# Cached attention with a gated MLP: steps and sums at other positions, first casts and one weight scaling on ScalarE, final adds but the last on GpSimd

## The chip, the cores and the metric

One core of a Trainium2 chip. The metric is device time of one launch in microseconds; of several runs the median is given. All instructions are written by hand for the five engines: TensorE (PE, with its weight loads as PEld), VectorE (DVE), ScalarE (ACT), GpSimd (POOL) and SyncE (SP), which issues the transfers. They meet only through semaphores, and each engine runs its own list in order: an instruction that waits holds everything behind it on that engine.

## The reference

```python
def _A_ref(x, k_cache, v_cache, wq, wo):          # Sq = Sk = 2048, D = 512, H = 32, Dh = 128
    q = (x @ wq).reshape(B, Sq, H, Dh).transpose(0, 2, 1, 3)
    scores = jnp.einsum("bhqd,bhkd->bhqk", q, k_cache) * (Dh ** -0.5)
    o = jnp.einsum("bhqk,bhkd->bhqd", softmax(scores), v_cache)
    return o.transpose(0, 2, 1, 3).reshape(B, Sq, H * Dh) @ wo

def _B_ref(x, W_gate, W_up, W_down):              # F = 1792
    gate = x @ W_gate
    gate = gate * (gate > 0)
    return (gate * (x @ W_up)) @ W_down

xn = layernorm(A_x)
return A_x + _A_ref(xn, ...) * silu(_B_ref(xn, ...))
```

## The kernel before

The work is 32 heads times 4 query quarters Q of 512 rows: 128 **blocks** b = 4h + Q. A block has 8 **pairs** p of two key tiles of 128. For each pair TensorE makes two score tiles (L1248, "S", 512 columns each) into PSUM, ScalarE takes their exponent in one instruction of 128x1024 (L1260, `PT`), and three pairs later TensorE multiplies `PT` with V (L1357, "PV", eight matmuls of 129 columns, the last column sums the exponents). (b, p) names a place in this sequence. At the end of a block VectorE makes a reciprocal of the sums (L1277) and the normalized output `Onorm` (L1280). The next block's first PV matmul writes the same PSUM banks and waits for that `Onorm`.

PSUM beside the two PV banks is a ring of three slots of two banks. Each S pair takes a slot until its exponent is done. All other products of TensorE ("M items", emitted by `emit_M`) take a slot too, until their results have been read. `plan` says at which (b, p) an M item stands; `side` does the same for VectorE work without TensorE, and `later`/`defer(n, fn)` runs a function n pairs later. These tables, filled by hand-written rules, are the whole order; within one engine the code's order is the run's order.

The M items are:

- `emit_qp` (L815, cast L822): query projections of heads 0 and 1. Those of head 0 stand ahead of the first block, those of head 1 in blocks 0 and 1.
- `emit_st` (L871, VectorE L876, L883): query projections of the later heads, two heads a time (`pr`), in a Strassen scheme of four steps for each half. Its weights are first scaled (L835) and summed (L843 to L848) on GpSimd by `emit_sw(pr)`.
- `emit_gu` (L935, L941): gate and up products of query quarters 1 and 3, in blocks 2 to 12, with weights scaled on ScalarE (L589) and summed on GpSimd (L594 to L599, `SG`). GpSimd also makes ReLU and product of the results (L911, L913).
- `emit_d` (L994, L1003) with sums `emit_hs` (L718 to L727): the down product in four steps, for Q = 1 in blocks 12 and 13.
- `emit_os` (L1131, L1149): output projection of a group g of four heads, four steps for each of four q, in the 16 blocks from b0 = 16(g + 1); sums `emit_ox` (L1100 to L1108, `OX`) feed it. Group 6 is the last one done this way (b0 = 112). Its step 3 also adds two results (L1196, L1198) and hands four output rows of 128 to `base_queue`. `emit_base` (L1225, L1230) then folds gate and residual into them, at the places of `base_at`.
- `emit_final_tile` (L1391): output projection of the last four heads for row tile n = 0 to 15. VectorE multiplies with the gate (L1399), adds (L1415), and SP writes the tile out (L1420). Tiles 0 to 7 stand in blocks 126 and 127, tiles 8 to 15 behind or between the last PV matmuls. The last block's normalization is split by bank (L1300, L1305 on ScalarE, L1311), and its result is transposed on TensorE (L1329).

LB = 124 is the first block of the last head.

Of the kernel before, what the change touches and what calls it, by code (L numbers as in the profile page):

```python
# [8 lines left out]
ALU = mybir.AluOpType  # L9
# [43 lines left out]
def bass_recurrent_scan__mha_block_cached__glu_gated_reglu__prompt_kernel(  # L53
# [35 lines left out]
    WSC = 512.0  # L89
# [26 lines left out]
    with ExitStack() as es:  # L116
# [691 lines left out]
        def emit_qp(h, Q, bank):  # L808
            qs = slice(Q * NQ, (Q + 1) * NQ)
            _wait(pe, wq_tok(0))  # L810
            if h == 0 and Q == 0:
                _wait_all(pe, xt_ready[0])
            ins = None
            for c in range(DC):
                ins = pe.matmul(ps_r[:, bank, :], Wq_sb[0][:, c, h, :], xnT[:, c, qs],  # L815
                                start=(c == 0), stop=(c == DC - 1))
            qtok = sem_qp.sig(ins)
            if h == 1 and Q == QB - 1:
                qp_done_tok[0] = qtok
            dst = qt_take(h, Q)  # L820
            _wait(dve, qtok)
            etok = sem_qpe.sig(dve.tensor_copy(dst, ps_r[:, bank, :]))  # L822
            qt_ready[(h, Q)] = etok
            return etok
# [3 lines left out]
        def emit_sw(pr):  # L828
# [5 lines left out]
            wflat = W[:].rearrange("p c i e -> p (c i e)")  # L834
            k = sem_sw.sig(pool.tensor_scalar(wflat, wflat, WSC, None, op0=ALU.mult))  # L835
            sw_tok[(pr, 0)] = k
# [273 lines left out]
        def emit_os(g, q, step, *banks):  # L1110
# [83 lines left out]
            if g == NG - 2:  # L1194
                _wait_all(dve, [k1, k2])
                t = sem_opa.sig(dve.tensor_tensor(c22, c22, c21, ALU.add))  # L1196
                _wait_all(dve, [t, os_tok[(q, "12")]])
                t = sem_opa.sig(dve.tensor_tensor(c12, c12, c22, ALU.add))  # L1198
                base_queue.extend((m, t) for m in (n, n + 1, NH + n, NH + n + 1))
            return [k1, k2]  # L1200
# [180 lines left out]
        def emit_final_tile(n, bank):  # L1381
# [8 lines left out]
            for hh in range(G):  # L1390
# [8 lines left out]
                dve.scalar_tensor_tensor(fin_tmp[fb], ps_r[:, bank, 0:D], 1.0 / (OSC * YSC), g_sb[:, n, :],  # L1399
                                         op0=ALU.mult, op1=ALU.mult))  # L1400
            flush_final_add()
            fin_pending.append((n, fb, mtok))
            return mtok
# [3 lines left out]
        def flush_final_add():  # L1407
            if not fin_pending:
                return
            n, fb, mtok = fin_pending.pop()  # L1410
            Q, j = divmod(n, 4)
            _wait(dve, mtok)
            _wait(dve, base_done[n])
            ftok = sem_opa.sig(
                dve.tensor_tensor(g_sb[:, n, :], s_acc[:, n, :], fin_tmp[fb], ALU.add))  # L1415
            fin_free[fb] = ftok
# [16 lines left out]
        for g in range(NG - 1):  # L1433
            b0 = (g + 1) * GB
            for i in range(16):
                it = (emit_os, 1 if i % 4 == 3 else 2, g, i // 4, i % 4)
                if g < NG - 2 or i < 10:
                    osteps[b0 + i] = it
                else:
                    at(b0 + 10 + (i - 10) // 2, 4 * (i % 2), it)  # L1440
            for c in range(2):
                for i in range(4):
                    side.setdefault((b0 + 7 * c, 2 + i), []).append((emit_ox, g, c, i))
        gu_n = [len(gu_seq)]

        def gu_items(n):
# [4 lines left out]
        dplan = {2: ((0, 2), (0, 5), (1, 2), (1, 5)),  # L1451
                 1: ((12, 3), (13, 1), (13, 3), (13, 6)),
                 3: ((14, 3), (15, 1), (15, 3), (15, 6))}
# [11 lines left out]
        for b in range(NBLK):  # L1465
# [10 lines left out]
            if 0 < pr < NPR:  # L1476
                c, step = r // 4, r % 4
                q = (emit_st, 1 if step == 3 else 2, pr, c, step)
                first, second = (o, q) if step == 3 and o else (q, o)
                at(b, 0, first)  # L1480
                if second:
# [5 lines left out]
        base_at += [(LB - 1 + k // 2, 2 + k % 2) for k in range(4)]  # L1487
        base_at += [(LB + 1, 1 + k) for k in range(4)]
        for bb, pp in base_at:
# [103 lines left out]
```

## Time and profile before

| | |
|---|---|
| median of 3 runs | 1262.67 us (1262.57 to 1262.78) |
| the profiled execution | 1260.62 us |
| its span, first to last instruction | 1259.3 us |
| busy: PE / ACT / DVE / POOL | 1246.5 / 1018.4 / 686.5 / 275.0 us |
| granted TensorE clock, mean | 0.999 |

A row of the timeline gives start and duration in us, engine, line, operation, tiles, shapes, a count of instructions merged into the row, and in brackets the idle time of the engine ahead of it with what ended it. Matmuls are pipelined: a matmul's duration is longer than the distance to the next one, so rows overlap. Sections of the span: the first gate and up products to about 68 us, attention with the rest of the MLP to about 250 us, attention with projections to 1245 us, and the last tiles behind that.

### The profile page before, as it was taken

What the parts mean: (1) busy time and instruction counts of PE and PEld (TensorE: products, weight loads), DVE (VectorE), ACT (ScalarE), POOL (GpSimd) and SP (SyncE); (2) the same over time, 40 slices, a digit from 0 to 9 for tenths busy, and PEclk for the clock granted to TensorE, in tenths of its full rate; (3) what the DMA queues carried; (4) which work ended last, traced back from release to release, by engine and by line L of the source; (5) the groups of instructions that cost most, each with busy time, mean ns of one, the idle gap of its engine ahead of it and who ended that gap; (6) DMA issues with size and microseconds to landing.
All of it is one profiled execution on the core that took longest, in us unless ns stands there. A gap on an engine that the chain in (4) does not pass through costs nothing.

```text
span 1259.3 us, 28894 instructions
## 1 busy us (share of the span) xinstructions
PE 1246.5 (99%) x12399; PEld 868.8 (69%) x12399; DVE 686.5 (55%) x1174; ACT 1018.4 (81%) x1105; POOL 275.0 (22%) x247
## 2 busy tenths in 40 slices
PE   9999999999999999999999999999999999999998
PEld 5466566777777777777777777777777777777774
DVE  6667677665454444454444545454544454456776
ACT  4356777668888888888888888888888888888884
POOL 2423999510401040100401040102110040100000
PEclk9999999999999999999999999999999999999999
DMA  9712341322223322333222223333223222333212
GB/s 272 154 31 35 70 78 31 51 39 38 44 50 57 68 58 49 60 64 59 52 37 45 59 55 52 60 64 60 52 56 68 56 37 40 52 81 68 68 31 76
DMA packets 250686, 78.02 MB, mean 62 GB/s; under 512 B 226240, under 2 KB 250560, under 8 KB 250560
## 3 DMA queue, kind: packets, MB, share of 16 engines
q1 hardware_dynamic: 249888, 75.79, 31.8%
q8 instruction: 98, 1.61, 0.5%
q10 hardware_dynamic: 672, 0.39, 0.1%
q14 instruction: 28, 0.23, 0.1%
HBM read 38.54 MB, written 2.10 MB: 32 GB/s over the span
## 4 chain that ended last, share of the span: by engine, by line
PE 93%; POOL 2%; DVE 2%; SPq 1%; issue 1%; ACT 1%; DMA 0%; DVEq 0%; POOLq 0%; ACTq 0%
PE ps_acc L1357 36%; PE ps_r L1248 34%; PE ps_r L871 7%; PE ps_r L1131 7%; PE ps_r L935 3%; PE ps_r L994 3%; PE ps_r L656 1%; PE ps_r L660 1%; PE ps_r L815 1%; PE ps_r L1391 1%; POOL hT L913 0%; ACT PT L1260 0%; SPq L521 0%; POOL xn_sb L409 0%; DVE WX L1399 0%
## 5 line engine op out<-in xcount | busy, mean ns | idle before, releaser
L1260 ACT ACTIVATE PT<-ps_r 128x1024 bf16<-128x1024 f32 x1024 | 970.0, 1029 | 170.3 <-PE ps_r L1248 169.8
L1357 PEld LDWEIGHTS ps_acc<-V_sb,PT 128*128 128x128 bf16 x8192 | 604.9, 98 | 220.1 <-ACT PT L1260 18.0
L1357 PE MATMUL ps_acc<-V_sb,PT 128*128 128x129 bf16 x8192 | 749.3, 220 | 1.9 <-DVE Onorm L1280 1.3
L1248 PE MATMUL ps_r<-QT_sb,KT_sb 128*128 128x512 bf16 x2048 | 727.0, 379 | 0.2 <-DVE QT_sb L822 0.2
L1149 DVE TENSOR_TENSOR s_acc<-s_acc,ps_r 128x512 f32<-128x512 f32 x264 | 167.6, 682 | 179.8 <-PE ps_r L1131 179.8
L835 POOL TENSOR_SCALAR Wq_sb<-Wq_sb 128x1024 bf16<-128x1024 bf16 x15 | 41.5, 2769 | 676.1 <-DMA Wq_sb<-in_A_wq_dram 676.1
L1248 PEld LDWEIGHTS ps_r<-QT_sb,KT_sb 128*128 128x128 bf16 x2048 | 187.9, 98 | 1.5 <-DVE QT_sb L822 0.7
L1277 DVE RECIPROCAL rz_sb<-ps_acc 128x4 f32<-128x4 f32 x127 | 23.1, 182 | 199.8 <-PE ps_acc L1357 199.5
L1280 DVE TENSOR_TENSOR Onorm<-ps_acc,rz_sb 128x512 bf16<-128x512 f32 x127 | 87.8, 691 | 4.4
L876 DVE TENSOR_TENSOR QT_sb<-cu,ps_r 128x512 bf16<-128x512 f32 x60 | 41.2, 687 | 85.0 <-PE ps_r L1248 79.8
L871 PE MATMUL ps_r<-xn_sb,SW 128*128 128x512 f16 x180 | 48.6, 379 | 0.0
L1131 PE MATMUL ps_r<-WX,OX 128*128 128x256 f16 x336 | 45.8, 273 | 0.0
L876 DVE TENSOR_TENSOR cu<-cu,ps_r 128x512 f32<-128x512 f32 x60 | 41.2, 687 | 0.0
L1131 PEld LDWEIGHTS ps_r<-WX,OX 128*128 128x128 f16 x336 | 32.9, 98 | 9.8
L876 DVE TENSOR_TENSOR QT_sb<-cv,ps_r 128x512 bf16<-128x512 f32 x60 | 38.3, 680 | 0.0
L1073 POOL TENSOR_SCALAR Wo_sb<-Wo_sb 128x2048 bf16<-128x2048 bf16 x7 | 37.7, 5391 | 0.6
L871 PEld LDWEIGHTS ps_r<-xn_sb,SW 128*128 128x128 f16 x180 | 17.6, 98 | 21.3 <-ACT PT L1260 0.2
L871 PE MATMUL ps_r<-xnT,Wq_sb 128*128 128x512 bf16 x120 | 30.8, 379 | 0.0
L616 ACT ACTIVATE gr_sb<-ps_r 128x512 bf16<-128x512 f32 x27 | 15.7, 593 | 16.7 <-PE ps_r L656 16.0
L1131 PE MATMUL ps_r<-Wo_sb,OT_store 128*128 128x256 bf16 x224 | 29.0, 273 | 0.0
L911 POOL TENSOR_SCALAR gB<-gB 128x512 bf16<-128x512 bf16 x14 | 20.8, 1484 | 32.3 <-DVE gB L941 32.3
L1131 PEld LDWEIGHTS ps_r<-Wo_sb,OT_store 128*128 128x128 bf16 x224 | 21.9, 98 | 8.5
(148 smaller groups left out, 925.1 us busy)
## 6 DMA issues: line engine op xcount, KB each, us to landing
V_sb<-in_A_v_cache_dram SPq DMA_DIRECT2D x32, 512.0 KB, 4.8
Wq_sb<-in_A_wq_dram SPq DMA_DIRECT2D x16, 256.0 KB, 3.3
Wo_sb<-in_A_wo_dram SPq DMA_DIRECT2D x8, 512.0 KB, 3.7
xr_sb<-in_A_x_dram SPq DMA_DIRECT2D x16, 128.0 KB, 2.1
OT_store<-Onorm SPq DMA_TRANSPOSE x127, 2.5
Wd_sb<-in_B_W_down_dram SPq DMA_DIRECT2D x1, 1792.0 KB, 13.6
W<-in_B_W_gate_dram SPq DMA_DIRECT2D x14, 128.0 KB, 2.4
W<-in_B_W_up_dram SPq DMA_DIRECT2D x14, 128.0 KB, 2.8
```

Of the source, the lines that this page charges most:

```text
L835: k = sem_sw.sig(pool.tensor_scalar(wflat, wflat, WSC, None, op0=ALU.mult))
L871: ins = pe.matmul(ps_r[:, bank, :], L(i), R(i), start=(i == 0), stop=(i == HC - 1))
L876: return sem_qpe.sig(dve.tensor_tensor(dst, a, ps_r[:, bank, :], op))
L935: ins = pe.matmul(ps_r[:, bank, :], L(i), R(i), start=(i == 0), stop=(i == HC - 1))
L994: ins = pe.matmul(ps_r[:, bank, j * DH:(j + 1) * DH], L(i), R(i), start=(i == 0 and j == 0), stop=(i == HF - 1 and j == 1))
L1073: k = sem_wx.sig(pool.tensor_scalar(wflat, wflat, WOSC, None, op0=ALU.mult))
L1131: ins = pe.matmul(ps_r[:, bank, j * DH:(j + 1) * DH], L(i), R(i), start=(i == 0 and j == 0), stop=(i == GH - 1 and j == 1))
L1149: t = dve.tensor_tensor(names[k], names[k], view(bank), op)
L1248: ins = pe.matmul(ps_r[:, 2 * s + tt, :], KT_sb[h % 2][:, t * 128:(t + 1) * 128], QT_sb[qt_slot[(h, Q)]][:], start=True, stop=True)
L1260: act.activation(PT[pb][:], ps_r[:, 2 * s:2 * s + 2, :], ACTF.Exp, scale=scale if h < 2 else scale / WSC)
L1280: dve.tensor_tensor(Onorm[ob][:], o_ap, rz_sb[:].to_broadcast([128, 4, Dh]), ALU.mult))
L1357: ins = pe.matmul(o_ap, PT[pb][:, tt, j * 128:(j + 1) * 128], V_sb[vb][:, t, 0:VW], start=(t == 0 and j % 2 == 0), stop=(t == KT - 1 and j ...
```

## The change

Eight edits. Head 0's projections of Q = 1 and 3 are cast on ScalarE instead of VectorE. The scaling of the weights of pr = 2 moves from GpSimd to ScalarE. The last group's two result sums (L1196, L1198) are deferred by one pair. Its steps of q = 3 stand at (123, 0), (124, 0), (125, 0), (125, 4) instead of (123, 0), (123, 4), (124, 0), (124, 4). `emit_ox` of the second half starts one pair earlier in every group. In block 13 the down product's second step changes place with the projection step: (13, 0) and (13, 2) instead of (13, 1) and (13, 0). The last four base sums stand at (125, 6), (125, 7), (126, 2), (126, 6) instead of (125, 1) to (125, 4). The final adds run on GpSimd, except that of tile 15, and directly behind their own multiply instead of behind the next one.

```diff
@@ emit_qp
-            _wait(dve, qtok)
-            etok = sem_qpe.sig(dve.tensor_copy(dst, ps_r[:, bank, :]))
+            if h == 0 and Q % 2 == 1:
+                _wait(act, qtok)
+                etok = sem_gua.sig(act.copy(dst, ps_r[:, bank, :]))
+            else:
+                _wait(dve, qtok)
+                etok = sem_qpe.sig(dve.tensor_copy(dst, ps_r[:, bank, :]))
@@ emit_sw
-            k = sem_sw.sig(pool.tensor_scalar(wflat, wflat, WSC, None, op0=ALU.mult))
+            if pr == 2:
+                _wait(act, wq_tok(pr))
+                k = sem_w2s.sig(act.activation(wflat, wflat, ACTF.Copy, scale=WSC))
+            else:
+                k = sem_sw.sig(pool.tensor_scalar(wflat, wflat, WSC, None, op0=ALU.mult))
             sw_tok[(pr, 0)] = k
             _wait(pool, k)
@@ emit_os, step 3
             if g == NG - 2:
-                _wait_all(dve, [k1, k2])
-                t = sem_opa.sig(dve.tensor_tensor(c22, c22, c21, ALU.add))
-                _wait_all(dve, [t, os_tok[(q, "12")]])
-                t = sem_opa.sig(dve.tensor_tensor(c12, c12, c22, ALU.add))
-                base_queue.extend((m, t) for m in (n, n + 1, NH + n, NH + n + 1))
+                def finish():
+                    ...
+                defer(1, finish)
@@ emit_final_tile, flush_final_add
+            fin_pending.append((n, fb, mtok))
             flush_final_add()
-            fin_pending.append((n, fb, mtok))
...
-            _wait(dve, mtok)
-            _wait(dve, base_done[n])
-            ftok = sem_opa.sig(
-                dve.tensor_tensor(g_sb[:, n, :], s_acc[:, n, :], fin_tmp[fb], ALU.add))
+            eng, sem = (dve, sem_opa) if n == NT - 1 else (pool, sem_hp)
+            _wait(eng, mtok)
+            _wait(eng, base_done[n])
+            ftok = sem.sig(eng.tensor_tensor(g_sb[:, n, :], s_acc[:, n, :], fin_tmp[fb], ALU.add))
@@ the tables
-                    at(b0 + 10 + (i - 10) // 2, 4 * (i % 2), it)
+                    at(b0 + (10, 10, 11, 12, 13, 13)[i - 10], 4 * (i in (11, 15)), it)
...
-                    side.setdefault((b0 + 7 * c, 2 + i), []).append((emit_ox, g, c, i))
+                    side.setdefault((b0 + 7 * c, (2, 1)[c] + i), []).append((emit_ox, g, c, i))
...
-                 1: ((12, 3), (13, 1), (13, 3), (13, 6)),
+                 1: ((12, 3), (13, 0), (13, 3), (13, 6)),
...
-                at(b, 0, first)
+                at(b, 2 if b == 13 else 0, first)
...
-        base_at += [(LB + 1, 1 + k) for k in range(4)]
+        base_at += [(LB + 1, 6), (LB + 1, 7), (LB + 2, 2), (LB + 2, 6)]
```

The changed kernel's lines are numbered 8 higher than the old ones from L843 on and 10 higher from L1225 on. First place: VectorE in blocks 124 to 126. Before, from the last two results of group 6 on; `Onorm_75` is block 124's output, `Onorm_76` that of block 125, L1225 and L1230 are one base sum:

```order
L1149 TENSOR_TENSOR s_acc_111<-s_acc_111,ps_r 128x2x256 x2
L1196 TENSOR_TENSOR s_acc_111<-s_acc_111 128x2x256
L1198 TENSOR_TENSOR s_acc_111<-s_acc_111 128x2x256
L1277 RECIPROCAL rz_sb_73<-ps_acc 128x4
L1280 TENSOR_TENSOR Onorm_75<-ps_acc,rz_sb_73 128x512
L1225 TENSOR_SCALAR s_acc_111<-s_acc_111,g_sb 128x512
L1230 TENSOR_TENSOR s_acc_111<-s_acc_111,xr_sb_116 128x512
```

and now, up to block 126's first two final tiles (L1409 is the old L1399):

```order
L1287 RECIPROCAL rz_sb_73<-ps_acc 128x4
L1290 TENSOR_TENSOR Onorm_75<-ps_acc,rz_sb_73 128x512
L1157 TENSOR_TENSOR s_acc_111<-s_acc_111,ps_r 128x2x256 x5
L1205 TENSOR_TENSOR s_acc_111<-s_acc_111 128x2x256
L1207 TENSOR_TENSOR s_acc_111<-s_acc_111 128x2x256
L1235 TENSOR_SCALAR s_acc_111<-s_acc_111,g_sb 128x512
L1240 TENSOR_TENSOR s_acc_111<-s_acc_111,xr_sb_116 128x512
L1235 TENSOR_SCALAR s_acc_111<-s_acc_111,g_sb 128x512
L1240 TENSOR_TENSOR s_acc_111<-s_acc_111,xr_sb_116 128x512
L1287 RECIPROCAL rz_sb_73<-ps_acc 128x4
L1290 TENSOR_TENSOR Onorm_76<-ps_acc,rz_sb_73 128x512
L1409 TENSOR_SCALAR WX_115<-ps_r,g_sb 128x512 x2
```

The results of q = 3 and their sums have moved behind block 124's output, and two base sums now stand ahead of block 125's. In the part before, four base sums and then block 125's reciprocal follow the rows shown.

Second place: ScalarE in block 4, from the scaling of gate and up weights into `W_67` to that into `W_68`. Before:

```order
L589 ACTIVATE W_67_84<-W_67_84 128x1024
L1260 ACTIVATE PT<-ps_r 128x1024 x4
L589 ACTIVATE W_68_85<-W_68_85 128x1024
```

and now (L1270 is the old L1260):

```order
L589 ACTIVATE W_67_84<-W_67_84 128x1024
L1270 ACTIVATE PT<-ps_r 128x1024 x2
L841 ACTIVATE Wq_sb<-Wq_sb 128x1024
L1270 ACTIVATE PT<-ps_r 128x1024 x2
L589 ACTIVATE W_68_85<-W_68_85 128x1024
```

The scaling stands between the second and the third exponent; on GpSimd its place between the sums `SG_87` and `SW_79` is now empty.

Third place: VectorE from tile 8's multiply to the end of the last block's normalization. Before:

```order
L1399 TENSOR_SCALAR WX_115<-ps_r,g_sb 128x512
L1415 TENSOR_TENSOR g_sb<-s_acc_111,WX_115 128x512
L1399 TENSOR_SCALAR WX_115<-ps_r,g_sb 128x512
L1415 TENSOR_TENSOR g_sb<-s_acc_111,WX_115 128x512
L1300 RECIPROCAL rz_sb_73<-ps_acc 128x2 x2
L1311 TENSOR_TENSOR Onorm_78<-ps_acc,rz_sb_73 128x256
```

and now from tile 4's multiply to VectorE's end, with the six adds between tile 4 and tile 9 gone:

```order
L1409 TENSOR_SCALAR WX_115<-ps_r,g_sb 128x512 x6
L1310 RECIPROCAL rz_sb_73<-ps_acc 128x2 x2
L1321 TENSOR_TENSOR Onorm_78<-ps_acc,rz_sb_73 128x256
L1409 TENSOR_SCALAR WX_115<-ps_r,g_sb 128x512 x6
L1425 TENSOR_TENSOR g_sb<-s_acc_111,WX_115 128x512
```

More of the change, by code (lines that the diff above doesn't have):

```diff
@@ L1194, in emit_os @@
             if g == NG - 2:
-                _wait_all(dve, [k1, k2])
-                t = sem_opa.sig(dve.tensor_tensor(c22, c22, c21, ALU.add))
-                _wait_all(dve, [t, os_tok[(q, "12")]])
-                t = sem_opa.sig(dve.tensor_tensor(c12, c12, c22, ALU.add))
-                base_queue.extend((m, t) for m in (n, n + 1, NH + n, NH + n + 1))
+                def finish():
+                    _wait_all(dve, [k1, k2])
+                    t = sem_opa.sig(dve.tensor_tensor(c22, c22, c21, ALU.add))
+                    _wait_all(dve, [t, os_tok[(q, "12")]])
+                    t = sem_opa.sig(dve.tensor_tensor(c12, c12, c22, ALU.add))
+                    base_queue.extend((m, t) for m in (n, n + 1, NH + n, NH + n + 1))
+                defer(1, finish)
             return [k1, k2]
```

## Prediction

> **What bounds the kernel now.** I read the page first, then who waited for whom on TensorE, then the timeline around each of those waits.
>
> ```profile
> span 1259.3 us, 28894 instructions
> PE 1246.5 (99%) x12399; PEld 868.8 (69%) x12399; DVE 686.5 (55%) x1174; ACT 1018.4 (81%) x1105; POOL 275.0 (22%) x247
> PE ps_r L935 <- POOL SG L599: 3.0, 1, 3.0
> ```
>
> TensorE is the bound nearly everywhere. Busy alone would not say so, as matmuls overlap; that its waits are few and short does. The change touches no product, so all it can win is idle time of TensorE ahead of its last matmul and the tail behind it. What counts is therefore each single wait, and what comes late next once it is gone.
>
> One rule for reading them. A 512-column matmul is shown as 0.38 us, but four take 1.03 (second row below), so they start every (1.03 - 0.38) / 3 = 0.216 us. An idle time in brackets starts only where the modelled end lies; the loss is larger by 0.38 - 0.216 = 0.16. I add 0.16 to each bracket.
>
> **First casts.**
>
> ```profile
> 70.43 2.47 DVE L822 CAST QT_sb<-ps_r 128x512 bf16<-128x512 f32 x4
> 71.74 1.03 PE L1248 MATMUL ps_r<-QT_sb,KT_sb 128*128 128x512 bf16 x4
> 72.37 2.86 ACT L1260 ACTIVATE PT<-ps_r 128x1024 bf16<-128x1024 f32 x3 [4.32 <-PE ps_r L1248]
> 72.96 1.09 PE L1248 MATMUL ps_r<-QT_sb,KT_sb 128*128 128x512 bf16 x4 [0.20 <-DVE QT_sb L822]
> 74.36 0.82 PE L815 MATMUL ps_r<-xnT,Wq_sb 128*128 128x512 bf16 x3 [0.31 <-ACT PT L1260]
> L616 ACT ACTIVATE gr_sb<-ps_r 128x512 bf16<-128x512 f32 x27 | 15.7, 593 | 16.7 <-PE ps_r L656 16.0
> ```
>
> The third S pair waits 0.36 us for four casts that run one behind the other to 72.90; a first exponent starts at 72.37, one PE-to-engine step of 0.41 behind the second S tile (71.74 + 0.216). With Q = 1 and 3 on ScalarE (0.59 each by L616) that wait goes: Q = 2 ends on VectorE before 71.8 and Q = 3, whose last matmul starts 0.216 ahead of S, runs 71.93 to 72.52; S wants the slot at 72.60. But the projections at 74.36 wait for the second exponent, and exponents follow each other on ScalarE. Q = 3's cast now stands ahead of the first one and lets it start at about 72.42. So the chain from the first exponent decides, TensorE waits 0.36 us less at one place and more at the next two, and the sum is **+0.05** (0 to +0.15).
>
> **The scaling of pr = 2.**
>
> ```profile
> Wq_sb<-in_A_wq_dram SPq DMA_DIRECT2D x16, 256.0 KB, 3.3
> 129.46 0.58 SPq L335 DMA_DIRECT2D Wq_sb<-in_A_wq_dram  x1
> 131.50 2.18 ACT L1260 ACTIVATE PT<-ps_r 128x1024 bf16<-128x1024 f32 x2
> 134.53 1.02 ACT L1260 ACTIVATE PT<-ps_r 128x1024 bf16<-128x1024 f32 x1 [0.86 <-PE ps_r L1248]
> L589 ACT ACTIVATE W<-W 128x1024 bf16<-128x1024 bf16 x14 | 14.8, 1057 | 3.2 <-DMA W<-in_B_W_up_dram 3.2
> 136.11 2.77 POOL L835 TENSOR_SCALAR Wq_sb<-Wq_sb 128x1024 bf16<-128x1024 bf16 x1
> 138.97 0.67 POOL L843 TENSOR_TENSOR SW<-Wq_sb 128x256 f16<-128x256 bf16 x1
> 149.79 0.38 PE L935 MATMUL ps_r<-xn_sb,SG 128*128 128x512 f16 x1 [3.03 <-POOL SG L599]
> ```
>
> The one large wait is 3.19 us. GpSimd's list runs without a gap from before 136 to the sums (`SG`) that TensorE wants at 149.79 - 3.19 = 146.60, so every microsecond taken out of it arrives there whole. What goes is L835 with its semaphore, 138.97 - 136.11 = 2.86. That leaves a wait of 0.33. On ScalarE the scaling has the shape of L589, 1.06 us, and stands behind the second exponent, which ends at 131.50 + 2.18 = 133.68, in a hole of 0.86; the pitch of such instructions is about 0.1 shorter than their duration, so the next exponent is late by 0.1 at most, and its reader comes three pairs later. Its data land at 129.46 + 3.3 = 132.8, 0.9 us early; a later landing would hold up the exponents behind it, which are then wanted by the ring within a microsecond. The cost on ScalarE I take at nothing, **-2.86** in all (-3.19 to -1.9, the end where landing slips by a microsecond).
>
> **Block 13.**
>
> ```profile
> 231.01 3.22 PE L994 MATMUL ps_r<-Wd_sb,hT 128*128 128x256 bf16 x28
> 237.33 1.16 DVE L727 TENSOR_TENSOR HS_sb<-hT,HS_sb 128x1024 f16<-128x1024 f16 x1
> 237.91 1.11 POOL L844 TENSOR_TENSOR SW<-Wq_sb 128x256 f16<-128x256 bf16 x1
> 238.62 0.69 DVE L1280 TENSOR_TENSOR Onorm<-ps_acc,rz_sb 128x512 bf16<-128x512 f32 x1
> 239.46 0.61 PE L1357 MATMUL ps_acc<-V_sb,PT 128*128 128x129 bf16 x8 [0.38 <-DVE Onorm L1280]
> ```
>
> PV can start 0.84 behind the start of `Onorm` (238.62 to 239.46), and two projection matmuls cover too little: 0.54 us lost. Now 28 down matmuls (3.06 us) stand there, and the wait goes. What is late next is the ring: the projection at (13, 2) and the down step at (13, 3) lie in neighbouring pairs, and the latter takes the slot of the S pair just ahead. From that S pair's second tile to the down step TensorE has 0.216 + 0.43 + 0.45 + 0.43 = 1.53 us of other work, an exponent needs 0.41 + 1.02 and a further 0.26, since the pair before it, without an M item, ends its S only 0.66 earlier and exponents follow each other by 0.92 ((2.86 - 1.02) / 2 by the row at 72.37). So 0.2 comes back: **-0.33** (-0.54 to 0).
>
> **`OX` a pair earlier, sums a pair later.**
>
> ```profile
> 1171.79 1.28 DVE L1149 TENSOR_TENSOR s_acc<-s_acc,ps_r 128x512 f32<-128x512 f32 x2 [1.73 <-PE ps_r L1131]
> 1174.44 0.68 DVE L1105 TENSOR_TENSOR OX<-OX,OT_store 128x1024 f16<-128x1024 f16 x1
> 1175.16 0.69 DVE L1108 TENSOR_TENSOR OX<-OT_store,OX 128x1024 f16<-128x1024 bf16 x1
> 1176.82 0.39 PE L1357 MATMUL ps_acc<-V_sb,PT 128*128 128x129 bf16 x4 [0.66 <-ACT PT L1260]
> ```
>
> This wait of 0.82 is put down to an exponent, but VectorE's list ran without a gap up to the `Onorm` that PV needs. L1105 now falls into the idle 1.73 ahead of L1149, which takes 1175.16 - 1174.44 = 0.72 out of the list, and the pause of a dependent step (0.12) goes between L1105 and L1108. The reciprocal then comes no later than the PV results allow: **-0.8** (-0.82 to -0.7).
>
> **Blocks 124 to 126.**
>
> ```profile
> 1214.78 0.60 PE L1131 MATMUL ps_r<-WX,OT_store 128*128 128x256 f16 x4
> 1217.49 0.69 DVE L1198 TENSOR_TENSOR s_acc<-s_acc 128x512 f32<-128x512 f32 x1
> 1218.53 0.18 DVE L1277 RECIPROCAL rz_sb<-ps_acc 128x4 f32<-128x4 f32 x1 [0.34 <-PE ps_acc L1357]
> 1219.35 0.68 DVE L1225 SCALAR_TENSOR_TENSOR s_acc<-s_acc,g_sb 128x512 f32<-128x512 f32 x1
> 1219.58 0.39 PE L1357 MATMUL ps_acc<-V_sb,PT 128*128 128x129 bf16 x4 [0.88 <-DVE Onorm L1280]
> 1220.68 0.68 DVE L1225 SCALAR_TENSOR_TENSOR s_acc<-s_acc,g_sb 128x512 f32<-128x512 f32 x1
> 1226.44 0.59 PE L1248 MATMUL ps_r<-QT_sb,KT_sb 128*128 128x512 bf16 x2
> 1228.60 0.62 PE L1357 MATMUL ps_acc<-V_sb,PT 128*128 128x129 bf16 x8
> ```
>
> Block 125 starts with no M item, so TensorE waits the bare 1.04 us for `Onorm`. Now eight matmuls of group 6 stand there, as at the other block ends, and this goes: -1.04. But the last step, with its sums, moves from (124, 4) to (125, 4), and two base sums now stand between these sums and block 125's reciprocal. Counted from the last step's first matmul (1214.78 before), the sums' second add starts 2.71 later and ends its turn at 3.43; two base sums take 2 x (1220.68 - 1219.35) = 2.66; the reciprocal comes at 6.1 instead of 3.75, PV may start 1.05 behind it, at 7.15 (1218.53 to 1219.58). TensorE reaches block 126's S at 3.55 and its PV, past the first two final tiles, 1228.60 - 1226.44 = 2.16 later, at 5.71. So a **new wait of about 1.4 us** stands at the start of block 126. The edit gives -1.04 + 1.4 = **+0.4** (-1.04 if VectorE gets through in time, +0.6 if it takes 0.2 longer).
>
> **The last tiles.**
>
> ```profile
> 1249.57 0.38 PE L1329 MATMUL ps_r<-ident,Onorm 128*128 128x128 bf16 x4 [0.60 <-ACT Onorm L1305]
> 1243.74 0.69 DVE L1399 SCALAR_TENSOR_TENSOR WX<-ps_r,g_sb 128x512 bf16<-128x512 f32 x1 [2.78 <-PE ps_r L1391]
> 1250.85 0.69 DVE L1399 SCALAR_TENSOR_TENSOR WX<-ps_r,g_sb 128x512 bf16<-128x512 f32 x1 [0.43 <-PE ps_r L1391]
> 1256.26 1.28 DVE L1415 TENSOR_TENSOR g_sb<-s_acc,WX 128x512 bf16<-128x512 f32 x2
> 1257.57 0.33 SPq L1420 DMA_DIRECT2D out_dram<-g_sb  x1
> L913 POOL TENSOR_TENSOR hT<-gA,uA 128x512 f16<-128x512 bf16 x14 | 16.2, 1155 | 1.2
> ```
>
> The transposes wait 0.76 us for the last normalization, which waits on VectorE behind two multiplies and two adds; without the adds (0.60 of list each, 1.28 less 0.68, what such a step takes by L1225) it starts up to 1.2 earlier, and the wait goes: -0.76. Behind it VectorE is the bound today: 16 multiplies and 16 adds by turns. Now the multiplies keep TensorE's pace, one tile in 4 x 0.216 = 0.865 us, and GpSimd adds. The trace has no f32 add on GpSimd; nearest is L913, the same 512 columns in two-byte types, 1.155 (pitch 1.13). Below that nothing speaks; above, if bytes set the price, a 1024-column add in two-byte types, extrapolated from 0.67 for 256 columns and 1.155 for 512, is 2.13. I take 1.13, since rates seem to go by columns. Tile 11's multiply, at 1250.85 - 0.76 = 1250.09, ends at 1250.8; four adds (11 to 14) end at 1255.3. Tile 15's add on VectorE reads two SBUF tensors, as L727 did above when it took 1.16 and L844 beside it 1.11 instead of 0.67; I add 0.3 for that. SP then issues tile 14 (0.33) and about 0.4 later tile 15, at 1256.1 instead of 1257.57: -1.5 for both, thus **-0.7** for the tail beyond the transposes (+1.4 at 1.48, +7.3 at 2.13).
>
> The Trainium skill speaks against this edit: its page "GPSIMD Engine Reference", section "Engine selection", puts elementwise work on VectorE, with GpSimd about half as fast in two-input adds. The rows agree on the price (1.155 against 0.68); going by the rule, the adds would stay and the 0.7 be lost, but here it is two lists side by side against one.
> The same page, section "Specifications", says that GpSimd shares its SBUF interfaces with VectorE when that reads two SBUF inputs. The rows L727 and L844 agree; nothing here shows whether a multiply that reads one of its inputs from PSUM is free of it, but L913's mean of 1.155 was taken while such combines ran on VectorE.
>
> **Sum.** 0.05 - 2.86 - 0.33 - 0.8 + 0.4 - 0.76 - 0.7 = -5.0 us against the profiled span of 1259.3, thus 1254.3, or 1255.6 for a profiled execution (1260.6 with what lies around the span). The median of the runs is 2.05 above that execution; I carry the difference to it: 1262.67 - 5.0 = **1257.7**. About 0.2% of it, 2.5 us, is what a measurement of this kernel can tell from no change.
>
> **Rivals.**
>
> *All waits go, none comes (11%).* Block 125's reciprocal would not stand behind the base sums in time, nor the ring hold the down step. For it: the list has slack at other block ends. Against it: the order on VectorE and the pitch of 1.33 a base sum. -5.0 - 1.4 - 0.2 = -6.6: 1256.1.
>
> *GpSimd's large gain is half eaten (12%).* `Wq_sb` lands a microsecond later than before, or the sums wait for something the long wait hid; exponents queue behind the scaling. TensorE then keeps 1 to 2 us of the 3.2. For it: a margin of 0.9 on one transfer. -5.0 + 1.5: 1259.2.
>
> *The adds on GpSimd become the end (6%, slower).* If f32 is paid by bytes, 2.13 each. From tile 6 on, whose multiply ends at 1243.74 + 0.69, nine adds end at 1263.6; 0.4 and the last transfer's 1.73 (1257.57 to the span's end) put the end at 1265.8, 6.5 later than today; with -3.5 from the edits before it this is +3.0: 1265.7. It decides from 1.8 us an add on for no gain, 2.1 for slower by 0.2%. Against it: L913's price, and that two-byte types of different kinds cost it the same. A middle price of 1.5 gives 1259.9.
>
> *The waits are not where the trace says (6%).* Each goes, and TensorE meets the exponents instead, as in the first edit: ScalarE is busy 81%. For it: brackets naming `PT`. Then -1 to -2: about 1261.
>
> **How the numbers follow.** My forecast with all its terms has 65%. Time 1257.7. The range, 1255.6 to 1260.6, holds it and the first two rivals and ends where GpSimd's add costs 1.6 or one term of 2.9 fails. Slower by over 0.2% is most of the third rival: 0.05. Within 0.2% are the fourth and what is left of the third and second: 0.09. Faster: 0.86.
>
> **What would show it.** In the profile after: no 3 us wait at L935 but one of 0.2 to 0.4; no wait at the first PV of blocks 13, 120 and 125 above 0.2; a new one of about 1.2 in the bracket at block 126's first PV, released by `Onorm`; the projections behind the first S pairs waiting for `PT` 0.7 to 0.9 in two steps; GpSimd's last adds at 1.1 to 1.2 us; the last transfer issued 5 us earlier. Adds of over 1.5 us, or a first-PV wait at block 126 that is missing, would make the sum wrong; exponents late around the moved scaling would make the largest term wrong.

## The result, and the profile after

| | before | after |
|---|---|---|
| median, six runs each | 1262.58 us (1261.37 to 1262.78) | 1256.28 us (1255.73 to 1256.70) |
| profiled execution / its span | 1260.62 / 1259.3 us | 1255.73 / 1254.1 us |

The changed kernel is faster: the ratio is 0.9951, with an interval of [0.9939, 0.9964]. The prediction was 1257.7 us, faster with 0.86. Its sum for the span was -5.0 us; the two spans differ by 5.2. The median fell by 6.3, and the 1.1 between the two is the most useful thing that this case has to show.

First the page of the changed kernel, then who waited for whom on TensorE (in total, times, longest, in us):

```profile
span 1254.1 us, 28671 instructions
PE 1234.5 (98%) x12173; PEld 868.8 (69%) x12399; DVE 681.7 (54%) x1157; ACT 1020.3 (81%) x1108; POOL 290.3 (23%) x261
PE ps_acc L1367 <- DVE Onorm L1290: 1.3, 1, 1.3
PE ps_r L815 <- ACT PT L1270: 0.3, 1, 0.3
PE ps_r L943 <- POOL SG L599: 0.2, 1, 0.2
```

TensorE's busy time can't be compared with before's: 226 of its matmul records are missing here (12,173 beside 12,399 weight loads). Its waits can. The 3.0 us for `SG` are down to 0.2, and the list is led by a wait for `Onorm`, at a place (block 126) where before had none. The timeline at the places that the prediction named, with the add of 0.16 to each bracket as there:

```profile
72.31 3.78 ACT L1270 ACTIVATE PT<-ps_r 128x1024 bf16<-128x1024 f32 x4
73.40 0.61 PE L1258 MATMUL ps_r<-QT_sb,KT_sb 128*128 128x512 bf16 x2 [0.25 <-ACT PT L1270]
74.31 1.04 PE L815 MATMUL ps_r<-xnT,Wq_sb 128*128 128x512 bf16 x4 [0.31 <-ACT PT L1270]
133.52 1.05 ACT L841 ACTIVATE Wq_sb<-Wq_sb 128x1024 bf16<-128x1024 bf16 x1
146.91 0.38 PE L943 MATMUL ps_r<-xn_sb,SG 128*128 128x512 f16 x1 [0.20 <-POOL SG L599]
241.55 0.38 PE L1258 MATMUL ps_r<-QT_sb,KT_sb 128*128 128x512 bf16 x1
241.99 0.28 PE L1002 MATMUL ps_r<-Wd,HS_sb 128*128 128x256 f16 x1
1221.28 0.69 DVE L1235 SCALAR_TENSOR_TENSOR s_acc<-s_acc,g_sb 128x512 f32<-128x512 f32 x1
1223.94 0.18 DVE L1287 RECIPROCAL rz_sb<-ps_acc 128x4 f32<-128x4 f32 x1
1224.99 0.61 PE L1367 MATMUL ps_acc<-V_sb,PT 128*128 128x129 bf16 x8 [1.25 <-DVE Onorm L1290]
```

Of the places in question, these waits are left: 0.41 and 0.47 for the first exponents, 0.36 for `SG`, 0.22 at block 13's down step (0.44 from the S tile ahead of it instead of 0.22), and 1.41 at block 126, where VectorE runs from 1221.28 without a gap through two base sums to the reciprocal. None is left at the first PV of blocks 13, 120 and 125, nor at the transposes. The end, where GpSimd now adds:

```profile
1246.16 5.60 POOL L1425 TENSOR_TENSOR g_sb<-s_acc,WX 128x512 bf16<-128x512 f32 x5 [0.77 <-DVE WX L1409]
1249.93 0.69 DVE L1409 SCALAR_TENSOR_TENSOR WX<-ps_r,g_sb 128x512 bf16<-128x512 f32 x1 [0.17 <-PE ps_r L1401]
1250.66 1.65 DVE L1425 TENSOR_TENSOR g_sb<-s_acc,WX 128x512 bf16<-128x512 f32 x1
1243.19 9.48 SPq L1430 DMA_DIRECT2D out_dram<-g_sb  x7
```

Five adds in 5.60 us are 1.12 each, as priced. The last add on VectorE took 1.65 us, not the 0.98 of the prediction.

### The profile page after: what moved, and what is told of

Same layout as the page of the kernel before. It is cut to its first block, busy times and chain, and to the rows that moved or that the text cites. A ratio compares the mean times of both kernels' runs of the same rounds, so it can differ in the third digit from the quotient of the medians.

```text
span 1254.1 us, 28671 instructions
## 1 busy us (share of the span) xinstructions
PE 1234.5 (98%) x12173; PEld 868.8 (69%) x12399; DVE 681.7 (54%) x1157; ACT 1020.3 (81%) x1108; POOL 290.3 (23%) x261
## 4 chain that ended last, share of the span: by engine, by line
PE 84%; ACT 10%; POOL 2%; issue 1%; SPq 1%; DVE 1%; DMA 0%; POOLq 0%; DVEq 0%; ACTq 0%
PE ps_acc L1367 34%; PE ps_r L1258 28%; ACT PT L1270 10%; PE ps_r L1139 6%; PE ps_r L879 6%; PE ps_r L943 3%; PE ps_r L1002 3%; PE ps_r L656 1%; PE ps_r L660 1%; PE ps_r L1401 1%; PE ps_r L815 1%; POOL hT L921 0%; SPq L521 0%; POOL xn_sb L409 0%; POOL gB L919 0%
## 5 line engine op out<-in xcount | busy, mean ns | idle before, releaser
L1270 ACT ACTIVATE PT<-ps_r 128x1024 bf16<-128x1024 f32 x1024 | 969.9, 1028 | 161.2 <-PE ps_r L1258 149.7
L1258 PE MATMUL ps_r<-QT_sb,KT_sb 128*128 128x512 bf16 x1831 | 652.7, 379 | 2.0 <-ACT PT L1270 0.2
L1157 DVE TENSOR_TENSOR s_acc<-s_acc,ps_r 128x512 f32<-128x512 f32 x264 | 167.7, 683 | 178.1 <-PE ps_r L1139 178.1
L843 POOL TENSOR_SCALAR Wq_sb<-Wq_sb 128x1024 bf16<-128x1024 bf16 x14 | 38.8, 2771 | 675.9 <-DMA Wq_sb<-in_A_wq_dram 675.9
L1425 POOL TENSOR_TENSOR g_sb<-s_acc,WX 128x512 bf16<-128x512 f32 x15 | 17.8, 1216 | 153.9 <-DVE WX L1409 153.9
```

What stands on the lines that cost most here:

```text
L1157: t = dve.tensor_tensor(names[k], names[k], view(bank), op)
L1258: ins = pe.matmul(ps_r[:, 2 * s + tt, :], KT_sb[h % 2][:, t * 128:(t + 1) * 128], QT_sb[qt_slot[(h, Q)]][:], start=True, stop=True)
L1270: act.activation(PT[pb][:], ps_r[:, 2 * s:2 * s + 2, :], ACTF.Exp, scale=scale if h < 2 else scale / WSC)
```

## Experiments

To compare traces I use one number throughout: the span less the start of the first exponent (1254.1 - 72.31 = 1181.8 for the changed kernel, 1259.3 - 72.37 = 1186.9 for before). It leaves out the part ahead of attention, in which one wait differs from execution to execution (more on it below). The spans are given to 0.1 us, so a difference of two of these numbers is good to about 0.1. Two profiles of the changed kernel agree that closely. The first casts stand partly ahead of this number's start, so they are read from the first S matmul instead.

| run | span less first exponent | median | before in the same comparison |
|---|---|---|---|
| before (first profile) | 1186.93 | | |
| before again | 1188.63 | 1263.04 | 1262.49 |
| before, wait filled | 1186.97 | 1261.32 | 1263.06 |
| after (first profile) | 1181.79 | 1256.28 | 1262.58 |
| after again | 1181.82 | 1256.96 | 1262.99 |
| scaling back on GpSimd | 1184.61 | 1260.62 | 1262.49 |
| casts back on VectorE | 1181.72 | 1256.59 | 1263.06 |
| `OX` back | 1182.40 | 1256.89 | 1263.06 |
| final adds back on VectorE | 1183.30 | 1257.55 | 1262.49 |
| base sums late | 1180.26 | 1255.12 | 1262.49 |
| last product in PSUM | 1181.66 | 1256.43 | 1263.06 |
| base sums late, two products in PSUM | 1179.83 | 1254.16 | 1262.99 |
| the same, sums of pr = 2 in block 8 | 1181.49 | 1255.70 | 1262.99 |

### Before, profiled again

No edit.

> The kernel before, unchanged, profiled a second time. The changed kernel's median is 6.3 us lower (1262.58 to 1256.28), but the spans of the two profiled executions differ by 5.2 only (1259.3 to 1254.1), and before's profiled execution (1260.62) lies 2.0 under its median while after's (1255.73) lies 0.6 under it. Theory: that 1.2 is no part of the change; this run's profile then shows the same single waits as the first one (3.19, 1.04, 0.82, 0.76, 0.54 us, each within 0.1), whatever its time is, and a longer execution is longer in the stretches between them or at the start. Rival: one of the waits is longer in an ordinary execution than in the one that was read (the 3.19 us above all, which hangs on GpSimd's list); its wait then shows 4 to 5 us here in an execution near 1262.5.

It was 1.70 us longer behind the first exponent, and the same waits stand there within 0.02 us. The windows (stretch, its length, busy time of PE, PEld, DVE, ACT and POOL, then the granted clock of TensorE, DMA share and GB/s) and TensorE's rows behind the 3.2 us wait:

```profile
151.00:153.00 2.00, 1.59 (x4) 0.59 (x5) 0.54 (x1) 0.00 (x0) 1.92 (x3) 0.59 0.00 0
153.00:155.00 2.00, 2.00 (x12) 1.27 (x11) 0.83 (x2) 0.01 (x1) 2.00 (x2) 0.55 0.00 0
155.00:157.00 2.00, 2.00 (x23) 1.40 (x22) 1.58 (x3) 1.05 (x2) 1.92 (x3) 1.00 0.00 0
151.41 1.87 PE L935 MATMUL ps_r<-xn_sb,SG 128*128 128x512 f16 x4 [3.04 <-POOL SG L599]
153.07 1.07 PE L1357 MATMUL ps_acc<-V_sb,PT 128*128 128x129 bf16 x8
154.79 0.60 PE L935 MATMUL ps_r<-xn_sb,SG 128*128 128x512 f16 x2
```

From 151.41 to about 154.8 the clock is halved: the four products take 1.87 us here and 1.02 in before's first profile, whose windows behind the same wait are at full clock:

```profile
149.79 1.02 PE L935 MATMUL ps_r<-xn_sb,SG 128*128 128x512 f16 x4 [3.03 <-POOL SG L599]
151.00:153.00 2.00, 2.00 (x20) 1.24 (x18) 1.63 (x4) 1.02 (x1) 1.92 (x3) 1.00 0.00 0
153.00:155.00 2.00, 2.00 (x23) 1.40 (x21) 1.23 (x3) 1.29 (x2) 1.92 (x3) 1.00 0.00 0
```

Half the clock for 3.4 us loses 1.7, which accounts for the 1.70. The other 1.6 us between the two spans (1262.6 and 1259.3) are the start-up of the last section.

So my theory was right that the waits are the same and the rival wrong that one is longer; but the surplus does lie at the wait, right behind it. The times of before show it as two groups. Of the 21 in this comparison ten lie from 1260.9 to 1261.6 at a mean clock of 0.999 to 1.000, eleven from 1262.5 to 1264.2 at 0.997 or 0.998. The profile that I read the sum from was of the lower group, the median of the upper.

### Before, with the wait filled

```diff
+            if (k, m) == (5, 6):
+                for _ in range(13):
+                    pe.matmul(ps_r[:, bank, :], W[:, 0, 0, :], xnT[:, 0, lo], start=True, stop=True)
             if m == 6:
                 _wait(pe, gu_tok[(k, "x")])
```

> The kernel before with 13 more matmuls of 512 columns in its 3.2 us wait, written to the bank that the waiting product overwrites: the wait is as long, but TensorE is busy for 2.8 us of it. The 21 times of before in the last comparison fall into two groups, ten from 1260.9 to 1261.6 and eleven from 1262.5 to 1264.2, and the second profile of before, a run of the upper group, shows a granted clock of 0.59 and 0.55 in the 3.4 us behind this wait. Theory: the idle time itself brings the clock down in about half of the executions, for 1.6 us. With TensorE kept busy the upper group is gone: every time within 1 us, a median near 1261.2, 1.3 under before. Rival: the clock drops there for another reason, or the groups come from the start-up: both groups stay, and the median is that of before.

```profile
146.55 2.97 PE L924 MATMUL ps_r<-xnT,W 128*128 128x512 bf16 x13
149.68 1.04 PE L938 MATMUL ps_r<-xn_sb,SG 128*128 128x512 f16 x4 [0.16 <-POOL SG L599]
151.00:153.00 2.00, 2.00 (x20) 1.17 (x17) 1.62 (x4) 1.02 (x1) 1.92 (x3) 1.00 0.04 8
```

The products start as late as ever, with 2.8 us of work that nobody needs ahead of them, and the median is 1261.32 against 1263.06 us, a ratio of 0.9991. Its interval, [0.9982, 1.0000], just reaches no change; the two groups tell more. Nine of its eleven times lie from 1260.6 to 1261.6. A tenth, 1262.45, ran at a clock of 1.000, so it lost its time elsewhere. The eleventh, 1264.11 at 0.998, looks like the upper group and stays unexplained. In before, ten of 14 on the same chip were above 1262.8. So it is the idle time that brings the clock down in nearly all of these executions; the one exception is open.

The Trainium skill, page "TensorE: Matmul & The Clock Gate", section "What's actually happening", has the array drop to half its clock after an idle window of about 3.4 us, by windows that run freely, and come back after one such window of work. Half the clock for 3.4 us and only in some executions agree with the rows above. The length does not: here 3.0 to 3.2 us of idle time were enough in more than half of the executions, and by the page's length there would have been no loss.

### The scaling back on GpSimd

```diff
-            if pr == 2:
-                _wait(act, wq_tok(pr))
-                k = sem_w2s.sig(act.activation(wflat, wflat, ACTF.Copy, scale=WSC))
-            else:
-                k = sem_sw.sig(pool.tensor_scalar(wflat, wflat, WSC, None, op0=ALU.mult))
+            k = sem_sw.sig(pool.tensor_scalar(wflat, wflat, WSC, None, op0=ALU.mult))
```

> The changed kernel with only the scaling of pr = 2 back on GpSimd. Theory: GpSimd's list has no gap from block 4 on, so 2.77 us and its semaphore arrive whole at the sums that TensorE waits for: the wait of 0.37 at the gate and up products becomes 3.2, the time rises by 2.8 us against the changed kernel (3.5 us under before). Rival: about half of the gain was eaten by ScalarE (exponents behind the scaling): then the 3.2 us wait is back, but the time rises by 1.3 to 2 only.

```profile
151.02 1.02 PE L939 MATMUL ps_r<-xn_sb,SG 128*128 128x512 f16 x4 [3.03 <-POOL SG L599]
```

The wait is 3.19 us again, and the profile 2.82 us longer than the changed kernel's (1184.61 - 1181.79). The rival, ScalarE eating half of the gain, is out. With the wait the wide spread is back: eleven times from 1258.9 to 1262.7 at clocks from 0.997 to 1.000, where kernels without it stay within 1.3 us.

### The first casts back on VectorE

```diff
-            if h == 0 and Q % 2 == 1:
-                _wait(act, qtok)
-                etok = sem_gua.sig(act.copy(dst, ps_r[:, bank, :]))
-            else:
-                _wait(dve, qtok)
-                etok = sem_qpe.sig(dve.tensor_copy(dst, ps_r[:, bank, :]))
+            _wait(dve, qtok)
+            etok = sem_qpe.sig(dve.tensor_copy(dst, ps_r[:, bank, :]))
```

> The changed kernel with all first casts back on VectorE. Theory: the chain of exponents decides there, not the casts; the 0.36 us wait for a cast is back, but the waits for the first exponents shrink by as much, and the four products of TensorE end at the same time within 0.1 us: no change of time that can be measured (0.05 less). Rival: the wait for the cast was the loss that the trace names: 0.36 us more, seen as a later start of the projections behind the first S pairs.

```profile
72.45 1.03 PE L1254 MATMUL ps_r<-QT_sb,KT_sb 128*128 128x512 bf16 x4
73.67 1.09 PE L1254 MATMUL ps_r<-QT_sb,KT_sb 128*128 128x512 bf16 x4 [0.20 <-DVE QT_sb L822]
75.08 0.60 PE L815 MATMUL ps_r<-xnT,Wq_sb 128*128 128x512 bf16 x2 [0.31 <-ACT PT L1266]
```

From the first S matmul to the projections there are 75.08 - 72.45 = 2.63 us; in the changed kernel 74.31 - 71.63 = 2.68, from the S row that comes first there:

```profile
71.63 1.52 PE L1258 MATMUL ps_r<-QT_sb,KT_sb 128*128 128x512 bf16 x6
```

The wait for a cast is back and nothing is lost. It was never a cost of its own: the same time is waited for an exponent instead. By these two rows the edit is worth +0.05, which is too little to be told from nothing.

### `OX` back

```diff
-                    side.setdefault((b0 + 7 * c, (2, 1)[c] + i), []).append((emit_ox, g, c, i))
+                    side.setdefault((b0 + 7 * c, 2 + i), []).append((emit_ox, g, c, i))
```

> The changed kernel with the sums OX of the second half of each group one pair later again, as before. Theory: VectorE's list, with these two sums in it, makes block 119's normalized output late; the wait of 0.82 us at block 120's first PV is back, and the time rises by 0.8 us. Rival: the wait there was for an exponent, as its row in the trace says, and went for another reason: no change. In the six earlier groups the sums have slack either way in both theories.

```profile
1172.32 0.69 DVE L1207 TENSOR_TENSOR s_acc<-s_acc 128x512 f32<-128x512 f32 x1
1172.93 0.17 DVE L1287 RECIPROCAL rz_sb<-ps_acc 128x4 f32<-128x4 f32 x1
1173.14 0.69 DVE L1290 TENSOR_TENSOR Onorm<-ps_acc,rz_sb 128x512 bf16<-128x512 f32 x1
1173.97 0.61 PE L1367 MATMUL ps_acc<-V_sb,PT 128*128 128x129 bf16 x8 [0.54 <-ACT PT L1270]
```

The wait is back with 0.70 us, and the time behind the first exponent is 0.61 longer. The row still names an exponent, but VectorE reaches the reciprocal without a gap and PV starts 0.83 behind the start of `Onorm`, as at block 13 before (0.84). The second profile of before settles it: there the same wait, with the same 0.66 in the bracket, is put down to `Onorm`:

```profile
1180.07 0.61 PE L1357 MATMUL ps_acc<-V_sb,PT 128*128 128x129 bf16 x8 [0.66 <-DVE Onorm L1280]
```

The name in the first profile's bracket was wrong, the list of VectorE right.

### The base sums late

```diff
-        base_at += [(LB + 1, 6), (LB + 1, 7), (LB + 2, 2), (LB + 2, 6)]
+        base_at += [(LB + 2, 1), (LB + 2, 2), (LB + 2, 6), (LB + 3, 2)]
```

> The changed kernel with the last four base sums at (126, 1), (126, 2), (126, 6) and (127, 2) instead of (125, 6), (125, 7), (126, 2) and (126, 6). Theory: the 1.42 us in front of block 126's first PV are the two base sums (2 x 1.33) that stand ahead of block 125's reciprocal on VectorE; without them the reciprocal starts at about 1222.0 in place of 1223.9 and the wait goes: 1.4 us less than the changed kernel. Rival: the reciprocal is held by the late step of group 6 (its four adds and two sums, which end at 1221.25) or by contention with GpSimd's adds in block 126; then the wait shrinks by half at most or comes back as 0.5 us or more at block 127's first PV: 0.7 us less or nothing.

```profile
1222.11 0.18 DVE L1287 RECIPROCAL rz_sb<-ps_acc 128x4 f32<-128x4 f32 x1 [0.37 <-PE ps_acc L1367]
1224.07 0.62 PE L1367 MATMUL ps_acc<-V_sb,PT 128*128 128x129 bf16 x8
```

The reciprocal now waits for TensorE, not TensorE for it, and block 126's PV has no wait: 1.53 us less, against a wait of 1.41 that is gone. The two base sums were the whole new wait.

### The final adds back on VectorE

```diff
-            fin_pending.append((n, fb, mtok))
             flush_final_add()
+            fin_pending.append((n, fb, mtok))
...
-            eng, sem = (dve, sem_opa) if n == NT - 1 else (pool, sem_hp)
+            eng, sem = dve, sem_opa
```

> The changed kernel with all final adds back on VectorE, each behind the next tile's multiply as before. Theory: the transposes wait 0.76 us again, and the chain of multiplies and adds on VectorE ends 0.8 us later behind TensorE's last matmul (4.2 us lay between that and the span's end in the changed kernel, 5.0 before): 1.6 us more than the changed kernel. The four base sums' adds in blocks 126 and 127, stretched to 1.0 to 1.5 us beside GpSimd's adds, return to 0.68 without a gain. Rival: the slowing that VectorE and GpSimd do to each other (0.68 to 1.65 at the last add) eats most of what the two lists win side by side; then the time rises by 0.6 us or less.

```profile
1246.51 0.38 PE L1339 MATMUL ps_r<-ident,Onorm 128*128 128x128 bf16 x4 [0.60 <-ACT Onorm L1315]
```

The transposes wait 0.76 us again, and the span behind the first exponent is 1.51 longer. The theory held, and contention ate little. This run undoes the engine and the order of the adds together; what each is worth alone was not tried. About 0.3 us of the gain is lost again outside the span (last section).

### The last product in PSUM

The main lines of the edit, shortened:

```diff
-                dve.scalar_tensor_tensor(fin_tmp[fb], ps_r[:, bank, 0:D], ...
+                dve.scalar_tensor_tensor(ps_r[:, bank, 0:D] if n == NT - 1 else fin_tmp[fb], ps_r[:, bank, 0:D], ...
...
+                                            last_bank[0] if n == NT - 1 else fin_tmp[fb], ALU.add))
```

> The changed kernel with the last tile's product left in PSUM in f32 instead of SBUF in bf16, so that VectorE's last add reads one of its inputs from PSUM. Theory: this add took 1.65 us in place of 0.68 because it reads both inputs from SBUF beside GpSimd's adds; with one in PSUM it takes 0.69 and ends at 1251.35 on the changed kernel's scale, and GpSimd's add of tile 14 (1251.76, perhaps 0.1 sooner) becomes the last: 0.4 to 0.6 us less in the time. Rival: GpSimd's traffic slows any VectorE instruction that reads f32 from SBUF; then the add takes 1.3 us or more and the time falls by 0.3 at most.

```profile
1249.49 2.26 POOL L1427 TENSOR_TENSOR g_sb<-s_acc,WX 128x512 bf16<-128x512 f32 x2
1250.66 0.69 DVE L1427 TENSOR_TENSOR g_sb<-s_acc,ps_r 128x512 bf16<-128x512 f32 x1
1250.66 1.92 SPq L1433 DMA_DIRECT2D out_dram<-g_sb  x3
```

The add takes 0.69 us beside the same GpSimd adds: with one input from PSUM it is free of them. (That input is f32 now and was bf16, but the multiplies, which also read one input from PSUM, take 0.69 there as well.) But the time behind the first exponent fell by about 0.1 only. GpSimd's add of tile 14 ends at 1249.49 + 2.26 = 1251.75, and SP issues tile 14 and then tile 15 behind it: the last issue ends at 1252.58 instead of 1252.67. I had taken the slowed add for the end; it was level with GpSimd's list.

### Both, and two products in PSUM

The base sums late, and in the edit above `n >= NT - 2` in place of `n == NT - 1`, in the choice of the engine too: GpSimd adds tiles 0 to 13. Beside it ran the changed kernel again and a third kernel that also moves the scaling and sums of pr = 2:

```diff
-                if pr < NPR:
+                if pr < NPR and pr != 2:
                     emit_sw(pr)
+            if pq == 4 and bq == 8:
+                emit_sw(2)
```

> The changed kernel, unchanged, beside the next two. Theory: without an idle stretch of TensorE over 1.5 us the granted clock stays at 1.0 throughout, so its times lie within about 1 us (1255.7 to 1256.7 so far) and no second group appears, on the same chip on which before shows two. Rival: the two groups of before have another cause; then some of these times lie 1.5 us or more above the rest.

> The changed kernel with the last base sums late as in the earlier experiment, and with both of the last tiles' products in PSUM and both adds on VectorE, each behind its multiply; GpSimd adds tiles 0 to 13. Theory: -1.4 for the wait at block 126; at the end GpSimd is done with tile 13 at 1250.6 on the changed kernel's scale, VectorE's last add, put off 0.4 by the add of tile 14, at 1251.65 instead of 1252.3, and the last transfer is issued 0.65 earlier: 2.1 us less than the changed kernel. Rival: what lies behind the last multiply is set by the one-by-one issues on SP (0.33 to 0.43 each), as the experiment with tile 15 alone suggests; then the tail gives 0.2 and the whole 1.6.

> The kernel above, with scaling and sums of pr = 2 in block 8 instead of block 4. Theory: TensorE's last 0.37 us at the gate and up products comes from the four sums (2.6 us of GpSimd) in block 4; in block 8 GpSimd's list has gaps of 1.3 us before and 0.7 and 2.6 us behind, and TensorE wants them in block 10 only: that wait goes, 0.3 us less. Rival: GpSimd is as far behind there; a wait of 0.5 us or more for SG or hT comes up in blocks 8 to 11, and it is no faster or slower.

The changed kernel's five times lie from 1256.37 to 1257.56 in one group, while seven of before's nine on that chip are in the upper one: the first theory holds. The better kernel's median is 1254.16 us, 2.8 under the changed kernel on the same chip and at 0.9933 [0.9921, 0.9946] of before. Behind the first exponent it is 1.96 shorter than the first profile of the changed kernel and 1.99 than the second (2.1 forecast). Of the rest of the 2.8, 0.3 lies around the span (last section); the other 0.5 is within the scatter of the start-up and was not followed up. Its last adds and issues:

```profile
1250.15 0.69 DVE L1409 SCALAR_TENSOR_TENSOR ps_r<-ps_r,g_sb 128x512 f32<-128x512 f32 x1
1250.88 0.69 DVE L1427 TENSOR_TENSOR g_sb<-s_acc,ps_r 128x512 bf16<-128x512 f32 x1
1249.31 2.61 SPq L1433 DMA_DIRECT2D out_dram<-g_sb  x4
```

The third kernel loses 1.66 us of that:

```profile
199.37 0.60 PE L943 MATMUL ps_r<-xn_sb,SG 128*128 128x512 f16 x2 [1.91 <-POOL SG L599]
```

The 0.36 us wait went and one of 2.07 came: GpSimd's list has less room for the four sums there than in block 4, and gaps before and behind do not say how much room a place has. The rival was right about the wait, and the kernel is slower, too. Its five times lie within 0.3 us of each other at a clock of 0.999 or more, so a wait of 2.1 us did not bring the clock down in these runs.

## Why the prediction was right, and where it was not

| term | forecast | measured |
|---|---|---|
| first casts | +0.05 | +0.05 (2.68 against 2.63) |
| scaling of pr = 2 | -2.86, 0.33 left | -2.83, 0.36 left; undone +2.82 |
| block 13 | -0.33, 0.2 back from the ring | -0.32, 0.22 back |
| `OX` earlier | -0.8 | wait gone; `OX` alone undone +0.61 |
| blocks 124 to 126 | +0.4, new wait 1.4 | +0.37, new wait 1.41; base sums later -1.53 |
| transposes and tail | -1.46 | undone +1.51 |
| sum | -5.0 | -5.1 (1186.93 to 1181.79) |

The block 13 line and the 1.04 us that went ahead of block 125 were read from the traces alone; no run undid them. `OX` put back costs 0.70 us of wait, where before had 0.82. In both, VectorE runs without a gap from the two adds at L1149 (L1157 in the changed kernel) to the reciprocal, in 3.98 us before (1171.79 to 1175.77) and 3.86 there (1169.07 to 1172.93): group 6's sums, a pair later, now stand in another order in this list, and that is the other 0.12.

**The price of GpSimd's add** was the largest doubt. It is 1.12 us where VectorE does not disturb it, by columns as L913 had it, not 2.13 by bytes. Tile 14 was forecast to end at 1255.3 less the 3.5 gained ahead of it, 1251.8, and ended at 1251.76. The rival of the slower kernel has nothing left.

**The mis-sized term** is the last add, with 0.3 for contention: the contention was 0.97 (1.65 against 0.68). It cost little, since the end lay on GpSimd's list as well: the run that removed it gained about 0.1.

**The step that failed** is the last one, "the median of the runs is 2.05 above that execution; I carry the difference". I took it for an offset of the runs; 1.7 us of it hung on the very wait that the change removes. Before's median lies in the group whose clock drops behind the wait, the profile in the other. Removing 2.83 us of idle time thus removed a further 1.7 in more than half of the executions. A second, smaller error went the other way: what lies around the span, which the prediction kept as it was, grew by 0.3 (1260.62 - 1259.3 = 1.32 before, 1255.73 - 1254.1 = 1.63 after). Together -5.1 - 1.7 + 0.3 = -6.5, against the 6.3 by which the median fell. So the sum over the span was right by its mechanism, and the forecast of the median missed by 1.4 us for a reason that was in none of its terms. The time of 1256.28 lies close to the rival "all waits go, none comes" (1256.1), but not for its reason: the wait at block 126 is there.

## What to carry to other kernels

Hold the profiled execution against the list of single times before you carry an offset: where the times of one kernel fall into two groups and the mean granted clock goes with them, look behind the longest wait of TensorE for a stretch at half clock, for it belongs to that wait's price. A wait is worth what comes late next, so follow the list of the engine that must deliver, in order, rather than the name in the bracket; that gave the new wait at block 126 to 0.03 us (7.15 - 5.71 = 1.44 forecast, 1.41 measured). When work is shared between two engines at the end of a kernel, speeding up the one that ends last may gain little until the other list is shortened too: here 0.1 us for an add that was 0.96 us shorter.

## What the runs showed of the hardware

**Idle time has a second price.** Behind an idle stretch of 3.2 us the profile of one execution shows about 3.4 us at half clock, 1.7 us of loss, and the mean clocks and times put 11 of 21 executions of one comparison with it. Kernels whose longest such wait was 1.4 or 2.1 us showed none of it.

The traces also show why only some executions pay. In all thirteen of them every stretch at full clock between two changes of the clock is a whole multiple of 3.4133 us: in the second profile of before 146.77 (43 times) ahead of the drop and 1105.92 (324 times) behind it; in the other profiles, from the first microseconds to a drop at the end, where TensorE has run out of work, 1245.87 to 1252.69 (365 to 367 times). So the clock seems to be decided at fixed points 3.413 us apart, by how busy TensorE was since the last one. Counted back from those changes, the stretches that hold the wait are these, in before's first and second profile, and below them one at the end of the kernel with pr = 2 in block 8:

```profile
147.78:151.19 3.41, 1.40 (x13) 0.96 (x14) 0.75 (x2) 0.15 (x1) 3.25 (x5) 1.00 0.00 0
147.95:151.36 3.41, 0.42 (x2) 0.00 (x0) 0.69 (x1) 1.59 (x2) 3.33 (x6) 1.00 0.05 11
1249.86:1253.27 3.41, 1.00 (x5) 0.27 (x3) 2.69 (x5) 0.00 (x0) 1.76 (x2) 1.00 0.53 180
```

Behind the first, with TensorE idle for 2.01 us of it, the clock stayed up; behind the other two, with 2.99 and 2.41 idle, it was halved. If the limit lies between 2.01 and 2.41 us, an estimate for a wait of 3.04 us at a random place is (3.41 + 3.04 - 2 x 2.41) / 3.41 = 48% to (3.41 + 3.04 - 2 x 2.01) / 3.41 = 71% of the executions. Of 55 executions of before in the last three comparisons, 35 (64%) are in the upper group (one of 1262.09 at a clock of 0.999 is counted with the lower). No run tried this rule.

**VectorE beside GpSimd.** In block 126, while GpSimd made its first two adds:

```profile
1225.52 2.72 POOL L1425 TENSOR_TENSOR g_sb<-s_acc,WX 128x512 bf16<-128x512 f32 x2 [145.44 <-DVE WX L1409]
1225.96 1.26 DVE L1235 SCALAR_TENSOR_TENSOR s_acc<-s_acc,g_sb 128x512 f32<-128x512 f32 x1
1227.26 1.53 DVE L1240 TENSOR_TENSOR s_acc<-s_acc,xr_sb 128x512 f32<-128x512 f32 x1
```

Instructions of VectorE that read two tensors from SBUF rose from 0.68 us to between 1.0 and 1.65, and these adds of GpSimd from 1.12 to 1.36. Instructions of VectorE with one input in PSUM kept 0.69: the multiplies all along, and the last add in the experiment. That settles what the prediction left open, and it agrees with the shared SBUF interfaces of the Trainium skill's page "GPSIMD Engine Reference", section "Specifications".

**Around the span.** In the seven profiles where GpSimd adds tile 14, the profiled execution is 1.63 to 1.69 us longer than its span; in the other six, where GpSimd stops at tile 13 or makes no final adds, it is 1.27 to 1.35 longer. So 0.3 us of the gain of the adds is given back there. The reason was not looked for.

**The start-up.** One wait ahead of attention differs from execution to execution; it was this in before's first and second profile:

```profile
PE ps_r L656 <- DVE hT L620: 0.3, 1, 0.3
PE ps_r L656 <- DVE hT L620: 2.1, 1, 2.1
```

In the thirteen profiles it lies between 0.3 and 2.1 us, and the first exponent starts between 72.31 and 73.97. Its cause was not followed up.
